# Decode attention with a gated MLP: part of the w_out matrix moved into a second transfer for partitions 0 to 31, and two products made 512 wide

## The chip, the cores and the metric

The kernel runs on one core of one Trainium2 chip. The metric is device microseconds (us) of one execution; lower is better. The kernel before was measured in three runs: 684.73, 684.85 and 684.87 us, median 684.85 us. One more execution was recorded by the hardware profiler; its own time is 684.74 us, and its span from the first to the last instruction is 682.9 us.

## The reference

One token for each of 8 batches goes through grouped-query attention over a cache, and the result is gated by a small MLP. All data are float32. Cut to what matters:

```python
xn = layernorm(x)                                # x: 8 x 512
q  = (xn @ wq)                                   # wq: 512 x 4096, 32 heads of 128
s  = softmax(q k^T / sqrt(128)) v                # k, v cache: 8 batches x 8 kv heads x 4096 x 128
s  = s.reshape(8, 4096) @ wo                     # wo: 4096 x 512
z  = gelu(xn @ w_in)                             # w_in: 512 x 1792, two halves z1, z2 of 896
g  = w_sp * layernorm(z2) + b_sp                 # scalars, since the sequence is 1 long
y  = (z1 * g) @ w_out                            # w_out: 896 x 512 = 7 blocks of 128 rows
out = x + s * silu(y)
```

The two caches hold 268 MB, nearly all of the 291 MB that one execution reads.

## The kernel before, in words

All large arrays come in over one queue, issued by SP in program order, into three slots of 64 KB in each of the 128 partitions (the pool `ring`). The order is: `w_mlp` (w_in and w_out side by side, 42 KB a partition), `wq`, then for each of the 8 kv heads two halves of k and two of v, each a full slot of 8 MB. SP issues a load as soon as the slot that it will overwrite has been read for the last time. Because the slots take turns, the second half of k for head 0 goes into the slot that `w_mlp` had, and its load waits until the MLP has written `gate` (line 182); the first half of v for head 0 waits for the last product with `wq`.

The second half of v of the last head comes in four pieces of 2 MB, and then `wo` in the pieces of `WO_PIECES` (line 29), counted in blocks m of 128 rows of `wo`: 16, 8, 4, 2, 1 and 1 blocks, so that little is left to compute when the last piece lands. Two small transfers go over a queue of their own, issued by ACT: `x` (8 rows of 2 KB) and `side` (128 rows of 520 bytes).

TensorE works in four column groups of 32 columns at a time (`R * g`), so that four products with few columns run side by side. For scores (line 212) and values (line 255) each product moves 512 columns of k or v past a small stationary matrix. Every matmul of float32 shows as two records in the profile. After a batch of values, DVE picks the diagonal blocks (`o_all`, line 258), adds them (`o_sb`, line 260), and `combine` (line 264) puts them into `po`, which is copied to `oT` (line 300).

The MLP (lines 121 to 182) runs while the first k loads are in flight. Its hidden vector lies in four groups of 32 partitions with 256 columns each; two transposes (line 168) and two copies turn it into `hT`, whose 7 blocks of 128 rows are multiplied by the 7 blocks of w_out, each in four column groups of 128 output columns (28 matmuls, line 174). The sigmoid of the result, times the result, is `gate`.

The final product (lines 303 to 307) takes 32 blocks of `wo`: for each block m four matmuls of 128 output columns, one in each column group g, all summed into the PSUM tile `acc`: 128 matmuls, 256 records. Then DVE multiplies by `gate`, adds `x` (from `side`), and SP stores 64 KB. The order of instructions within an engine is set by a planner when the program is built; it may put a `combine` ahead of the next batch of values.

Of the kernel before, what the change touches and what calls it, by code (L numbers as in the profile page):

```python
# [8 lines left out]
F32 = mybir.dt.float32  # L9
# [4 lines left out]
P = 128  # L14
B, D = 8, 512
HKV, REP, S, DH = 8, 4, 4096, 128
NK = D // P
G = 4
J = S // (G * P)
R = 32  # L20
FH = 896
FQ = 256
NB = FH // P
# [2 lines left out]
HALF = B // 2  # L26
UNIT = 2 * G * 512
SLOT = HALF * UNIT
WO_PIECES = [(0, 16), (16, 24), (24, 28), (28, 30), (30, 31), (31, 32)]


@with_exitstack
def tile_gqa_gmlp_decode(ctx: ExitStack, tc: tile.TileContext, x, side, kT, v, wq, wo,
                         w_mlp, out):
    nc = tc.nc
    const = ctx.enter_context(tc.tile_pool(name="const", bufs=1))
    ring = ctx.enter_context(tc.tile_pool(name="ring", bufs=3))
    work = ctx.enter_context(tc.tile_pool(name="work", bufs=1))
    small = ctx.enter_context(tc.tile_pool(name="small", bufs=2))
    ps_fix = ctx.enter_context(tc.tile_pool(name="ps_fix", bufs=1, space=bass.MemoryType.PSUM))  # L40
    ps = ctx.enter_context(tc.tile_pool(name="ps", bufs=2, space=bass.MemoryType.PSUM))

    def slot():
        return ring.tile([P, SLOT], F32, name="slot")
# [5 lines left out]
    nc.scalar.dma_start(side_sb, side)  # L50

    mlp_slot = slot()
    n_in, n_mlp = NK * 2 * FH, NK * 2 * FH + NB * D
    nc.sync.dma_start(mlp_slot[:, :n_mlp], w_mlp)
    w_in_sb = mlp_slot[:, :n_in].rearrange("p (k n) -> p k n", k=NK)
    w_out_sb = mlp_slot[:, n_in:n_mlp].rearrange("p (j d) -> p j d", j=NB)
    spare = [n_mlp]

    def from_slot(rows, n):
        lo = spare[0]  # L60
        spare[0] = lo + n
        return mlp_slot[:rows, lo:lo + n]
# [6 lines left out]
    ident = const.tile([P, P], F32, name="ident")  # L69
# [7 lines left out]
    same = const.tile([P, G, R], F32, name="same")  # L77
# [11 lines left out]

    sc = ps_fix.tile([P, 2, 512], F32, name="sc")  # L90
    o_ps = [ps_fix.tile([P, G, DH], F32, name=f"o_ps{i}") for i in range(2)]
    acc = ps_fix.tile([P, P], F32, name="acc")
    po_ps = ps_fix.tile([P, 2, B * REP], F32, name="po_ps")
    for t in (o_ps[0], o_ps[1], acc):
        nc.vector.memset(t, 0.0)

    def scratch(shape, name):
        t = ps.tile([P, 512], F32, name="scr")
        n = 1
        for s in shape[1:]:  # L100
            n *= s
        return t[:shape[0], :n]
# [16 lines left out]
    gate = const.tile([P, P], F32, name="gate")  # L119

    def mlp():
        z = from_slot(P, 2 * FQ).rearrange("p (a f) -> p a f", a=2)
        u = from_slot(P, 2 * FQ).rearrange("p (a f) -> p a f", a=2)
        pz = scratch([P, 2 * FQ], "pz")
        nc.vector.memset(pz, 0.0)
        for part in range(2):
            for k in range(NK):
                for g in range(G):
                    lo = g * FQ
                    n = min(FQ, FH - lo)  # L130
                    nc.tensor.matmul(pz[R * g:R * (g + 1), part * FQ:part * FQ + n], xnT[:, k, :],  # L131
                                     w_in_sb[:, k, part * FH + lo:part * FH + lo + n],
                                     start=(k == 0), stop=(k == NK - 1))
        zf, uf = z.rearrange("p a f -> p (a f)"), u.rearrange("p a f -> p (a f)")
        nc.vector.tensor_copy(zf, pz)
        nc.vector.tensor_mul(uf, zf, zf)
        nc.vector.tensor_scalar(uf, uf, 0.044715, 1.0, op0=ALU.mult, op1=ALU.add)
        nc.vector.tensor_mul(uf, uf, zf)
        nc.scalar.activation(uf, uf, AF.Tanh, scale=GELU_C)
        nc.vector.tensor_scalar(uf, uf, 1.0, 0.5, op0=ALU.add, op1=ALU.mult)  # L140
        nc.vector.tensor_mul(zf, uf, zf)

        def mean(src, name):
            part_sum = small.tile([P, 1], F32, name="part_sum")
            nc.vector.tensor_reduce(part_sum, src, op=ALU.add, axis=AX.X)
            pm = scratch([P, 1], "pm")
            nc.tensor.matmul(pm, same_all, part_sum, start=True, stop=True)
            t = small.tile([P, 1], F32, name=name)
            nc.vector.tensor_scalar(t, pm, 1.0 / FH, None, op0=ALU.mult)
            return t  # L150

        z1, z2 = z[:, 0, :], z[:, 1, :]
        mu = mean(z2, "mu")
        nc.vector.tensor_scalar(z2, z2, mu, None, op0=ALU.subtract)
        nc.vector.tensor_mul(u[:, 0, :], z2, z2)
        nc.vector.memset(u[(G - 1) * R:, 0, FH - (G - 1) * FQ:], 0.0)
        var = mean(u[:, 0, :], "var")
        nc.vector.tensor_scalar(var, var, EPS, None, op0=ALU.add)
        rs = small.tile([P, 1], F32, name="rs")
        nc.gpsimd.tensor_tensor(rs, var, neg_half, op=ALU.pow)  # L160
        nc.vector.tensor_scalar(z2, z2, rs, None, op0=ALU.mult)
        nc.vector.tensor_scalar(z2, z2, side_sb[:, P:P + 1], side_sb[:, P + 1:P + 2],
                                op0=ALU.mult, op1=ALU.add)
        nc.vector.tensor_mul(u[:, 1, :], z2, z1)
        hT = from_slot(P, 2 * P).rearrange("p (a s) -> p a s", a=2)
        for a in range(2):
            th = scratch([P, P], "th")
            nc.tensor.transpose(th, u[:, 1, a * P:(a + 1) * P], ident)
            nc.vector.tensor_copy(hT[:, a, :], th)
        py = scratch([P, P], "py")  # L170
        for j in range(NB):
            g0, a = divmod(j, 2)
            for g in range(G):
                nc.tensor.matmul(py[R * g:R * (g + 1), :], hT[:, a, R * g0:R * (g0 + 1)],  # L174
                                 w_out_sb[:, j, g * P:(g + 1) * P],
                                 start=(j == 0), stop=(j == NB - 1))
        e = from_slot(P, P)
        nc.vector.tensor_scalar(e, py, -1.0, 87.0, op0=ALU.mult, op1=ALU.min)
        nc.scalar.activation(e, e, AF.Exp)
        nc.vector.tensor_scalar(e, e, 1.0, None, op0=ALU.add)  # L180
        nc.vector.reciprocal(e, e)  # L181
        nc.vector.tensor_mul(gate, py, e)
# [22 lines left out]
    oT = const.tile([P, HKV, REP, B], F32, name="oT")  # L205
# [65 lines left out]
    def load_v(h, half, parts):  # L271
# [4 lines left out]
        return t.rearrange("p (i j e) -> p i j e", i=HALF, j=J)  # L276

    mlp()
    project_q(0)
    project_q(1)  # L280
    for h in range(HKV):
        for half in range(2):
            scores(h, half, load_k(h, half))
        pT = softmax(h)
        po = po_ps[:, h % 2]
        for half in range(2):
            last = h == HKV - 1 and half == 1
            v_sb = load_v(h, half, HALF if last else 1)
            if last:
                wo_slot = slot()  # L290
                for lo, hi in WO_PIECES:
                    nc.sync.dma_start(wo_slot[:, lo * D:hi * D], wo[:, lo * D:hi * D])
# [7 lines left out]
        nc.vector.tensor_copy(oT[:, h], po.rearrange("p (b r) -> p r b", r=REP))  # L300

    wo_sb = wo_slot.rearrange("p (m d) -> p m d", d=D)
    for m in range(HKV * REP):
        h, r = divmod(m, REP)
        for g in range(G):
            nc.tensor.matmul(acc[R * g:R * g + B, :], oT[:, h, r, :], wo_sb[:, m, g * P:(g + 1) * P],  # L306
                             start=(m == 0), stop=(m == HKV * REP - 1))

    res = const.tile([P, P], F32, name="res")
    nc.vector.tensor_mul(res, acc, gate)  # L310
# [37 lines left out]
```

## Time and profile before

| what | value |
|---|---|
| median of three runs | 684.85 us |
| time of the profiled execution | 684.74 us |
| its span | 682.9 us |
| busy PE, PEld, DVE | 373.4, 120.0, 172.1 us |
| data moved | 291.25 MB, mean 426 GB/s |
| share of queue q1 (all SP loads) in the time of the 16 DMA engines | 98.7% |
| product with wo (line 306), 256 records | 10.1 us busy, in the last 11 us |
| product with w_out (line 174), 56 records | 3.2 us busy, 32.6 to 35.8 us |
| store of the result, issue to landing | 1.6 us |

PE is TensorE's matmul row, PEld its weight loads, DVE the vector engine, SP the engine that issues the loads. In a group of instructions the columns are line, engine and operation, what is written and read, the shape, and the count; then busy time, mean duration in ns, and the idle time before them with what ended it. The clock that the throttle granted to TensorE is given in shares of full speed; in this kernel it is either 1.0 or 0.5, in stretches of 7 to 17 us.

The trace holds each DMA packet with its start, duration, size and queue, and each transfer's 16 completion events, one for each DMA engine. It does not name the engine of a packet. But the packets of one engine follow each other without a gap (the next starts 4 ns before the one before it ends), so that 16 chains can be followed from end to start through the span.

### The profile page before, as it was taken

How to read it: one execution, taken by the hardware profiler on the slowest of the kernel's cores; microseconds unless marked ns; L12 is line 12 of the kernel's file. 1: busy time of each engine (PE TensorE's matmuls, PEld its weight loads, DVE VectorE, ACT ScalarE, POOL GpSimd, SP SyncE). 2: the span in 40 equal slices, each digit the busy share in tenths (PEclk: the TensorE clock that was granted, in tenths of full speed). 3: DMA queues.
4: the chain of work that ended last, by engine and by line, in shares of the span. 5: the costliest groups of instructions: out<-in, count | busy, mean ns of one | idle time of the engine just before them, and what ended most of it. 6: DMA issues, size and time to landing. Idle time of an engine off the chain costs nothing.

```text
span 682.9 us, 6041 instructions
## 1 busy us (share of the span) xinstructions
PE 373.4 (55%) x2730; PEld 120.0 (18%) x2730; DVE 172.1 (25%) x370; ACT 13.5 (2%) x27; POOL 3.7 (1%) x11
## 2 busy tenths in 40 slices
PE   0455565447665455546665355556654454655676
PEld 0221121102111121112111011111211121111224
DVE  2440043302440033402431024401521024400441
ACT  0000000000000000000000000000000000000000
POOL 1000000000000000000000000000000000000000
PEclk9787768766777777777778777776777777766776
DMA  9999999999999999999999999999999999999996
GB/s 389 430 431 431 434 446 434 439 441 427 430 427 430 427 430 427 441 427 438 439 430 431 441 434 431 435 430 435 434 431 442 430 431 430 427 427 430 417 432 245
DMA packets 6521, 291.25 MB, mean 426 GB/s; under 512 B 728, under 2 KB 984, under 8 KB 1376
## 3 DMA queue, kind: packets, MB, share of 16 engines
q1 hardware_dynamic: 6336, 290.79, 98.7%
q8 instruction: 21, 0.34, 0.2%
q10 hardware_dynamic: 160, 0.08, 0.0%
q14 instruction: 4, 0.03, 0.0%
HBM read 290.80 MB, written 0.07 MB: 426 GB/s over the span
## 4 chain that ended last, share of the span: by engine, by line
DMA 72%; PE 19%; issue 4%; another core or an unknown queue 3%; DVE 2%; POOLq 0%; POOL 0%; ACT 0%; SPq 0%
DMA slot<-in_v 34%; DMA slot<-in_kT 33%; PE o_ps L255 9%; PE sc L212 9%; DMA slot<-in_wo 4%; PE po_ps L264 1%; PE scr L174 0%; DVE o_sb L260 0%; PE scr L243 0%; DMA x_sb<-in_x 0%; DVE o_all L258 0%; DVE nm L217 0%; DVE slot L181 0%; DVE p L238 0%
## 5 line engine op out<-in xcount | busy, mean ns | idle before, releaser
L212 PE MATMUL sc<-slot,qz 128*32 128x512 f32 x1024 | 147.8, 742 | 142.4 <-DMA slot<-in_kT 142.4
L255 PE MATMUL o_ps<-slot,pT 128*16 128x512 f32 x1024 | 154.0, 743 | 73.9 <-DMA slot<-in_v 73.9
L258 DVE TENSOR_TENSOR o_all<-o_ps,diag 128x512 f32<-128x512 f32 x64 | 44.2, 691 | 150.6 <-PE o_ps L255 150.5
L217 DVE TENSOR_REDUCE nm<-sc 128x1 f32<-128x1024 f32 x8 | 9.8, 1225 | 286.9 <-PE sc L212 286.9
L212 PEld LDWEIGHTS sc<-slot,qz 128*32 128x32 f32 x1024 | 36.0, 133 | 247.8 <-DMA slot<-in_kT 140.2
L260 DVE TENSOR_REDUCE o_sb<-o_all 128x128 f32<-128x512 f32 x64 | 67.9, 1061 | 2.2
L255 PEld LDWEIGHTS o_ps<-slot,pT 128*16 128x16 f32 x1024 | 30.0, 112 | 155.0 <-issue 105.4
L264 PE MATMUL po_ps<-fold,o_sb 128*128 128x4 f32 x128 | 25.0, 266 | 28.0 <-DVE o_sb L260 27.9
L264 PEld LDWEIGHTS po_ps<-fold,o_sb 128*128 128x128 f32 x128 | 19.4, 191 | 73.8 <-DVE o_sb L260 73.8
L243 PE MATMUL scr<-ident,p 128*128 128x128 f32 x64 | 15.2, 418 | 10.7 <-DVE p L238 10.7
L219 ACT ACTIVATE p<-sc,nm 128x1024 f32<-128x1024 f32 x8 | 8.9, 1114 | 584.5 <-DVE nm L217 584.5
L245 DVE COPY pT<-scr 128x128 f32<-128x128 f32 x64 | 13.9, 284 | 9.9 <-PE scr L243 9.9
L243 PEld LDWEIGHTS scr<-ident,p 128*128 128x128 f32 x64 | 12.3, 219 | 11.1 <-issue 11.1
L306 PE MATMUL acc<-slot,oT 128*8 128x128 f32 x256 | 10.1, 326 | 1.6 <-DMA slot<-in_wo 1.6
L131 PE MATMUL scr<-slot,xnT 128*32 128x256 f32 (+1 forms) x64 | 5.0, 451 | 10.7 <-DMA slot<-in_w_mlp 10.7
L222 PE MATMUL scr<-ident,nm 128*1 128x128 f32 x8 | 2.2, 270 | 10.9 <-DVE nm L217 10.9
L306 PEld LDWEIGHTS acc<-slot,oT 128*8 128x8 f32 x256 | 7.3, 105 | 4.2 <-DMA slot<-in_wo 2.2
L189 PE MATMUL scr<-slot,xnT 128*32 128x512 f32 x64 | 7.5, 609 | 0.0
L235 PE MATMUL scr<-wl,same 128*128 128x1 f32 x16 | 3.6, 297 | 6.2 <-DVE wl L233 6.2
L238 DVE TENSOR_SCALAR p<-p,w 128x1024 f32<-128x1024 f32 x8 | 6.0, 753 | 0.3
L131 PEld LDWEIGHTS scr<-slot,xnT 128*32 128x32 f32 x64 | 2.9, 138 | 12.4 <-issue 11.8
L201 DVE COPY qz<-scr 128x4 f32<-128x4 f32 x64 | 4.6, 152 | 1.5 <-PE scr L195 1.5
(74 smaller groups left out, 56.3 us busy)
## 6 DMA issues: line engine op xcount, KB each, us to landing
slot<-in_v SPq DMA_DIRECT2D x4, 2048.0 KB, 41.0
slot<-in_w_mlp SPq DMA_DIRECT2D x1, 5376.0 KB, 15.4
slot<-in_wo SPq DMA_DIRECT2D x1, 4096.0 KB, 38.5
slot<-in_wo SPq DMA_DIRECT2D x1, 2048.0 KB
slot<-in_wo SPq DMA_DIRECT2D x1, 1024.0 KB, 45.1
slot<-in_wo SPq DMA_DIRECT2D x1, 512.0 KB, 37.9
slot<-in_wo SPq DMA_DIRECT2D x2, 256.0 KB, 31.6
slot<-in_kT SPq DMA_DIRECT2D x16, 48.3
```

Source lines behind the costliest of these rows:

```text
L131: nc.tensor.matmul(pz[R * g:R * (g + 1), part * FQ:part * FQ + n], xnT[:, k, :], w_in_sb[:, k, part * FH + lo:part * FH + lo + n], start=( ...
L189: nc.tensor.matmul(pq[R * g:R * (g + 1), :], xnT[:, k, :], wq_sb[:, k, lo:lo + REP * DH], start=(k == 0), stop=(k == NK - 1))
L212: nc.tensor.matmul(sc[R * g:R * (g + 1), c, :], qz[:, h, b * R:(b + 1) * R], k_sb[:, i, c, g, :], start=(b == 0), stop=(b == B - 1))
L217: nc.vector.tensor_reduce(m, sc, op=ALU.max, axis=AX.XY, negate=True)
L219: nc.scalar.activation(p.rearrange("p j s -> p (j s)"), sc.rearrange("p c s -> p (c s)"), AF.Exp, bias=m, accum_out=l[:, h:h + 1])
L243: nc.tensor.transpose(t[:, j * P:(j + 1) * P], p[:, 4 * c + j, :], ident)
L245: nc.vector.tensor_copy(pT[:, 4 * c + j].rearrange("p b (g r) -> p g b r", g=G), t[:, j * P:(j + 1) * P].rearrange("p (g b r) -> p g b r", ...
L255: nc.tensor.matmul(of[R * c:R * c + G * REP, :], pT[:, j, b, :], v_unit[:, j], start=(j < G), stop=(j >= J - G))
L258: nc.vector.tensor_mul(o_all, o, diag[:, :, None].to_broadcast([P, G, DH]))
L260: nc.vector.tensor_reduce(o_sb, o_all.rearrange("p g d -> p d g"), op=ALU.add, axis=AX.X)
L264: nc.tensor.matmul(po[:, b * REP:(b + 1) * REP], o_sb, fold, start=True, stop=True)
L306: nc.tensor.matmul(acc[R * g:R * g + B, :], oT[:, h, r, :], wo_sb[:, m, g * P:(g + 1) * P], start=(m == 0), stop=(m == HKV * REP - 1))
```

## The change

There are three parts.

1. The weights of the MLP are split. `w_mlp` keeps w_in and the w_out blocks 0, 2, 4 and 6 (6 KB a partition fewer, in all 128 partitions). The blocks 1, 3 and 5 go into a new array `w_low` as quarters of 32 rows: 32 rows of 24 KB, written as 8 groups of 4 rows with 256 bytes of padding behind each group. One transfer issued by ACT, behind `x` and `side`, brings them to partitions 0 to 31. The bytes moved are the same.
2. The product with w_out is made 512 columns wide: one transpose and one copy for the four even blocks (4 matmuls), four transposes and one copy for the quarters (12 matmuls with 32 rows), summed in `pw`; the partial sums lie in four row groups and are copied to SBUF and folded by 4 matmuls with `same`. Some buffers of the MLP move from the slot to the tiles `p` and `pT`.
3. `wo` comes in seven pieces (8, 8, 8, 4, 2, 1, 1 blocks). The blocks 0 to 27 are multiplied 512 columns wide, one matmul for each block, four blocks side by side in the column groups; the sum is copied to SBUF and folded into `acc` by 4 matmuls. The last 4 blocks go the old way, two ahead of the fold and two behind it. `part` and `acc` reuse the PSUM of the scores.

```diff
-WO_PIECES = [(0, 16), (16, 24), (24, 28), (28, 30), (30, 31), (31, 32)]
+WO_PIECES = [(0, 8), (8, 16), (16, 24), (24, 28), (28, 30), (30, 31), (31, 32)]
+FOLDED = HKV * REP - REP
+QR = P // 4
+LOW_E = 8
+N_LOW = (NB - G) * 4 * D
...
-    n_in, n_mlp = NK * 2 * FH, NK * 2 * FH + NB * D
+    n_in, n_mlp = NK * 2 * FH, NK * 2 * FH + G * D
+    n_low = n_mlp + N_LOW
     nc.sync.dma_start(mlp_slot[:, :n_mlp], w_mlp)
...
+    nc.scalar.dma_start(mlp_slot[:QR, n_mlp:n_low],
+                        w_low[:, :P // (4 * LOW_E) * N_LOW].rearrange("e (i n) -> e i n", n=N_LOW))
...
-    for t in (o_ps[0], o_ps[1], acc):
+    for t in o_ps:
...
-        for a in range(2):
-            th = scratch([P, P], "th")
-            nc.tensor.transpose(th, u[:, 1, a * P:(a + 1) * P], ident)
-            nc.vector.tensor_copy(hT[:, a, :], th)
+        nc.tensor.transpose(th, u[:, 1, :P], ident)
+        nc.vector.tensor_copy(hT, th)
+        tl = scratch([QR, 4 * P], "tl")
+        for a in range(4):
+            nc.tensor.transpose(tl[:, a * P:(a + 1) * P], u[:, 1, P + a * QR:P + (a + 1) * QR], ident)
+        nc.vector.tensor_copy(hL.rearrange("p a s -> p (a s)"), tl)
+        pw = scratch([P, D], "pw")
+        for g in range(G):
+            nc.tensor.matmul(pw[R * g:R * (g + 1), :], hT[:, R * g:R * (g + 1)], w_out_sb[:, g, :],
+                             start=True, stop=(g == G - 1))
+        for a in range(4):
+            for g in range(NB - G):
+                nc.tensor.matmul(pw[R * g:R * (g + 1), :], hL[:, a, R * g:R * (g + 1)],
+                                 w_low_sb[:, g, a, :], start=False, stop=(a == 3))
+        nc.vector.tensor_copy(y_sb, pw)
         py = scratch([P, P], "py")
-        for j in range(NB):
-            g0, a = divmod(j, 2)
-            for g in range(G):
-                nc.tensor.matmul(py[R * g:R * (g + 1), :], hT[:, a, R * g0:R * (g0 + 1)],
-                                 w_out_sb[:, j, g * P:(g + 1) * P],
-                                 start=(j == 0), stop=(j == NB - 1))
+        for g in range(G):
+            nc.tensor.matmul(py[R * g:R * (g + 1), :], same[:, 0, :], y_sb[:, g * P:(g + 1) * P],
+                             start=True, stop=True)
...
-    for m in range(HKV * REP):
+    part, acc = sc[:, 0, :], sc[:, 1, :P]
+    for m in range(FOLDED):
         h, r = divmod(m, REP)
-        for g in range(G):
-            nc.tensor.matmul(acc[R * g:R * g + B, :], oT[:, h, r, :], wo_sb[:, m, g * P:(g + 1) * P],
-                             start=(m == 0), stop=(m == HKV * REP - 1))
+        nc.tensor.matmul(part[R * r:R * r + B, :], oT[:, h, r, :], wo_sb[:, m, :],
+                         start=(m < REP), stop=(m >= FOLDED - REP))
+    part_sb = work.tile([P, D], F32, name="part_sb", tag="p")
+    nc.vector.tensor_copy(part_sb, part)
+
+    def last_head(lo, hi):
+        for m in range(lo, hi):
+            h, r = divmod(m, REP)
+            for g in range(G):
+                nc.tensor.matmul(acc[R * g:R * g + B, :], oT[:, h, r, :], wo_sb[:, m, g * P:(g + 1) * P],
+                                 start=(m == FOLDED), stop=(m == HKV * REP - 1))
+
+    last_head(FOLDED, FOLDED + 2)
+    for g in range(G):
+        nc.tensor.matmul(acc[R * g:R * g + B, :], same[:, 0, :B], part_sb[:, g * P:(g + 1) * P],
+                         start=False, stop=False)
+    last_head(FOLDED + 2, HKV * REP)
...
+    w2 = c(B_w_out).reshape(NB, P, D)
+    rows = P // (4 * LOW_E)
+    low = np.zeros((LOW_E, rows * N_LOW + 64), np.float32)
+    low[:, :rows * N_LOW] = w2[1::2].reshape(NB - G, 4, LOW_E, rows, D).transpose(2, 3, 0, 1, 4).reshape(LOW_E, -1)
```

More of the change, by code (lines that the diff above doesn't have):

```diff
@@ L28 @@
 SLOT = HALF * UNIT
-WO_PIECES = [(0, 16), (16, 24), (24, 28), (28, 30), (30, 31), (31, 32)]
+WO_PIECES = [(0, 8), (8, 16), (16, 24), (24, 28), (28, 30), (30, 31), (31, 32)]
[3 more added lines that the diff above has]
+N_LOW = (NB - G) * 4 * D
 @with_exitstack
 def tile_gqa_gmlp_decode(ctx: ExitStack, tc: tile.TileContext, x, side, kT, v, wq, wo,
-                         w_mlp, out):
+                         w_mlp, w_low, out):
     nc = tc.nc
@@ L52, in tile_gqa_gmlp_decode @@
     mlp_slot = slot()
-    n_in, n_mlp = NK * 2 * FH, NK * 2 * FH + NB * D
+    n_in, n_mlp = NK * 2 * FH, NK * 2 * FH + G * D
+    n_low = n_mlp + N_LOW
     nc.sync.dma_start(mlp_slot[:, :n_mlp], w_mlp)
     w_in_sb = mlp_slot[:, :n_in].rearrange("p (k n) -> p k n", k=NK)
-    w_out_sb = mlp_slot[:, n_in:n_mlp].rearrange("p (j d) -> p j d", j=NB)
-    spare = [n_mlp]
+    nc.scalar.dma_start(mlp_slot[:QR, n_mlp:n_low],
+                        w_low[:, :P // (4 * LOW_E) * N_LOW].rearrange("e (i n) -> e i n", n=N_LOW))
+    w_out_sb = mlp_slot[:, n_in:n_mlp].rearrange("p (j d) -> p j d", j=G)
+    w_low_sb = mlp_slot[:QR, n_mlp:n_low].rearrange("p (j a d) -> p j a d", a=4, d=D)
+    spare = [n_low]
     def from_slot(rows, n):
@@ L91, in tile_gqa_gmlp_decode @@
     o_ps = [ps_fix.tile([P, G, DH], F32, name=f"o_ps{i}") for i in range(2)]
-    acc = ps_fix.tile([P, P], F32, name="acc")
     po_ps = ps_fix.tile([P, 2, B * REP], F32, name="po_ps")
-    for t in (o_ps[0], o_ps[1], acc):
+    for t in o_ps:
         nc.vector.memset(t, 0.0)
@@ L121, in mlp @@
     def mlp():
-        z = from_slot(P, 2 * FQ).rearrange("p (a f) -> p a f", a=2)
-        u = from_slot(P, 2 * FQ).rearrange("p (a f) -> p a f", a=2)
+        zu = work.tile([P, 4, FQ], F32, name="zu", tag="p")
+        z, u = zu[:, :2], zu[:, 2:]
+        hy = work.tile([P, 2 * D], F32, name="hy", tag="pT")
+        y_sb, hL = hy[:, :D], hy[:QR, D:].rearrange("p (a s) -> p a s", a=4)
         pz = scratch([P, 2 * FQ], "pz")
@@ L164, in mlp @@
         nc.vector.tensor_mul(u[:, 1, :], z2, z1)
-        hT = from_slot(P, 2 * P).rearrange("p (a s) -> p a s", a=2)
-        for a in range(2):
-            th = scratch([P, P], "th")
-            nc.tensor.transpose(th, u[:, 1, a * P:(a + 1) * P], ident)
-            nc.vector.tensor_copy(hT[:, a, :], th)
-        py = scratch([P, P], "py")
-        for j in range(NB):
-            g0, a = divmod(j, 2)
-            for g in range(G):
-                nc.tensor.matmul(py[R * g:R * (g + 1), :], hT[:, a, R * g0:R * (g0 + 1)],
-                                 w_out_sb[:, j, g * P:(g + 1) * P],
-                                 start=(j == 0), stop=(j == NB - 1))
+        hT = from_slot(P, P)
+        th = scratch([P, P], "th")
+        nc.tensor.transpose(th, u[:, 1, :P], ident)
[13 more added lines that the diff above has]
+        nc.vector.tensor_copy(y_sb, pw)
+        py = scratch([P, P], "py")
+        for g in range(G):
+            nc.tensor.matmul(py[R * g:R * (g + 1), :], same[:, 0, :], y_sb[:, g * P:(g + 1) * P],
+                             start=True, stop=True)
         e = from_slot(P, P)
@@ L336 @@
             c(B_w_in).reshape(NK, P, 2 * FH).transpose(1, 0, 2).reshape(P, NK * 2 * FH),
-            c(B_w_out).reshape(NB, P, D).transpose(1, 0, 2).reshape(P, NB * D)], axis=1),
+            w2[0::2].transpose(1, 0, 2).reshape(P, G * D)], axis=1),
+        "w_low": low,
     }
```

## The prediction

> **What bounds the kernel now.** I read the page's DMA slices and queues first, then the end of the chain of work that ended last, the timeline and clock of the last 25 us, SP's own waits, and last the single packets and completion events.
>
> ```profile
> span 682.9 us, 6041 instructions
> ...
> DMA  9999999999999999999999999999999999999996
> ...
> q1 hardware_dynamic: 6336, 290.79, 98.7%
> q8 instruction: 21, 0.34, 0.2%
> q10 hardware_dynamic: 160, 0.08, 0.0%
> q14 instruction: 4, 0.03, 0.0%
> ```
> ```profile
> 649.78 29.43 DMA slot<-in_wo
> 679.21 0.04 issue
> 679.25 0.45 PE acc L306 x8
> 679.70 0.02 issue
> 679.72 0.30 DVE res L310
> ```
>
> The DMA engines are busy in every slice, q1 alone for 98.7% of their time. The landing of the last wo piece at 679.21 sets the end; 8 TensorE records, two DVE operations and the store follow. A change can move only that landing or what is left behind it.
>
> The transfers give the cause of 679.21. A packet of 65,536 bytes takes 2.418 us on every engine, all span long (tenth to ninetieth percentile 2.418 to 2.427). Yet the 16 completions of the last wo piece come at 674.16, .22, .23, .34, .46, .56, .63 (seven engines), 677.36, .41, .61, .64, .74 (five) and 678.85, .90, 679.19, .21 (four). Followed packet by packet, the delays are the instruction packets of q8 and q14: a q8 packet (16,384 bytes) costs its engine 1.50 to 1.56 us, a q14 packet (8,192 bytes) 0.95 to 0.98. The q8 packets go round eight chains, two or three times each. The three q14 packets ahead of the end (47, 210 and 516 us) all fall on a ninth chain, which I call the odd one: 3.2 us late, completion 677.41. Seven chains get none.
>
> ```profile
> 667.33 0.59 PE L264 MATMUL po_ps<-fold,o_sb 128*128 128x4 f32 x2 [1.87 <-DVE o_sb L260]
> ...
> 669.31 9.70 PE L306 MATMUL acc<-slot,oT 128*8 128x128 f32 x248 [1.40 <-DMA slot<-in_wo]
> ...
> 679.25 0.40 PE L306 MATMUL acc<-slot,oT 128*8 128x128 f32 x8 [0.24 <-DMA slot<-in_wo]
> ```
> ```profile
> 669.30:674.40 5.10, 5.09 (x98) 3.63 (x101) 0.00 (x0) 0.00 (x0) 0.00 (x0) 0.50 0.96 392
> 674.40:677.90 3.50, 3.50 (x133) 3.10 (x124) 0.00 (x0) 0.00 (x0) 0.00 (x0) 1.00 0.49 192
> ```
>
> TensorE is nearly a second bound: it waits for wo from 667.9 to 669.31, then works without a break until 677.9, half of it at clock 0.50, and only the last four blocks wait for their data.
>
> **The transfer w_low.** It takes 3 blocks x 2 KB = 6 KB from each of the 128 rows of w_mlp: 8 rows an engine, 49,152 bytes. From the pitches of packets (65,536 bytes every 2.414 us, 32,768 every 1.21) an engine moves 27.2 bytes a ns, so every engine gains 1.81 us. The 768 KB come back in 32 rows. Which engines carry them? `x`, also 8 groups on ACT's queue, left 8 packets of 2,048 bytes and 8 completions on 8 engines. Five of these run straight into a first w_mlp packet and so can be placed: all five are chains without q8 packets. So I take the eight of `x` as the half that q8 leaves alone: the seven early chains and the odd one. If w_low takes the same eight, each gets 98,304 bytes, 3.61 us, plus 4 packets' gaps and a completion, 0.03: net +1.84 us; the other eight get -1.81.
>
> At the end: the seven land at 674.63 + 1.84 = 676.47 at the latest, the q8 chains at 679.21 - 1.81 = 677.40, the odd chain at 677.41 + 1.84 = 679.25. The odd chain takes the place of the slowest, 0.04 us behind it. The eight that were late gain 1.8 us and nobody is left to use it.
>
> A rule speaks against the transfer as such: the Trainium skill, "DMA: Bandwidth & Descriptors", section "Rules for kernel authors", asks for all 16 engines and warns that a small outermost dimension confines a transfer to few. By it the 1.84 us would be a loss, landing 681.05; the completions above show seven of the eight engines some 5 us early, so here the price is 0.04.
>
> **The piece of wo split in two.** 16 rows an engine of 16,384 bytes (0.610 pitch) for 8 of 32,768 (1.21): 9.76 - 9.68 = +0.08 us with the completion, on all engines; landing 679.33. SP issues one more load; these issues wait for transfers eight back:
>
> ```profile
> SPq L268 <- DVE gate L182: 36.1, 1, 36.1
> SPq L292 <- DMA slot<-in_v: 17.1, 3, 8.0
> ```
>
> With one piece more, the last one waits for the last v piece (659.55) and stands 18 us ahead of its data: nothing. The store, queued behind it on SP, waits for DVE anyway.
>
> **The MLP.** The w_out product becomes 10 sets of four (or three) records side by side. Values, also 512 wide, start such sets 0.44 us apart at clock 1.0 and 0.85 at 0.5, so 4.4 to 8.5 us for 3.21; copies of 0.69 (two of 512 columns), three more transposes and a fold add 1.5 to 2, and the low engines' w_mlp lands 1.5 to 1.9 us later. `gate` comes 4 to 10 us after its 38.11. Queued behind is SP's load of the second k half (the first line above) and everything that SP issues after it, and project_q on TensorE, so the first v load and the first scores also. The queue holds k's first half until 54.0: cover 15.9 us, above the upper end. From scores on each load has a slot's time, 19.3 us, in hand. Nothing reaches the end. DVE's instructions come out even (a memset and two copies against four copies), so its packets stay where they are.
>
> **The product with wo.** 256 records become 96; with the MLP's -13, 173 pairs or 346 TensorE instructions fewer. q8 packets come every 254 instructions in the mean (193 to 300 from one to the next), so one or two fewer of 21, at the very end: the one at 673.1 falls late or away, on a chain that has 1.8 us to spare then. Nothing.
>
> On TensorE a block costs the same: four records side by side, 0.109 us a set at clock 1.0 and 0.213 at 0.5 for 128 columns, two sets a block; 512 wide, two sets of 0.43 or 0.85 for four blocks. So 0.22 or 0.43 us a block either way. What changes is the order. Piece 0 to 8 (landing near 664.6) is there when values end at 667.95; 16 blocks at 0.43 end by 674.8; the next 8 (landed 674.4) by 676.5 at clock 1.0; blocks 24 to 27, landing near 676.8 on the odd chain, end at 677.75 with the pipeline. Then a new chain: part_sb, 128x512 from PSUM, 0.69 as line 135's copy, done 678.5; fold, 0.22, done 678.8, with blocks 28 and 29 (landing 678.0) ahead of it; block 30 (678.7) done 679.0; block 31 at 679.33. So 0.3 us are to spare, and from the landing on the tail is the old one, 0.45 us of TensorE and DVE and store unchanged: +0.0. At clock 0.5 through blocks 24 to 31: 676.8 + 1.8 + 0.75 + 0.43 + 0.86 = 680.6 against 679.8: +0.8, the upper end.
>
> **Sum.** 0.04 + 0.08 + 0.0 = +0.12 us on the profiled 684.74: 684.86. That run stands 0.11 below the median of 684.85, so the forecast is 685.0. I call within 0.2% (1.37 us) no change; a measurement of this kernel tells about that.
>
> **Rivals.**
> - Faster: the odd chain is not the last, because it is not among w_low's eight, or its three q14 packets spread over other engines. For: only five of `x`'s eight engines could be placed; the odd one is in by exclusion. Against: the q8 round has exactly eight members, and it is none of them. Then the q8 chains set the end at 677.40 + 0.08 = 677.48; blocks 24 to 27 land at 675, so TensorE keeps up; 684.74 - 1.73 = 683.0.
> - Slower, by the clock: it stays at 0.5 to the end. For: TensorE starts 1.4 us earlier into a stretch of 0.5 that began at 657.3. Against: that one already lasted 17.1 us, the longest of all. 24 blocks then end at 678.2, 27 at 679.9, part_sb 680.65, fold 681.1, block 31 at 682.0 against 679.70: 687.1. It decides once 1.0 comes later than about 680.
> - Slower, by the low half: w_low costs its engines over 3.1 us more (fewer than eight engines, or packets slower than 27.2 bytes a ns), or the odd chain gets one more instruction packet. On four engines the transfer costs 7.2 us instead of 3.6: 688.5; with low engines as late as the others, the full 1.84 us would show: 686.6. The completions speak against the one, and no row shows a slower packet past the first 3 us of the span. The 686.6 is what the Trainium skill's rule on all 16 engines, above, would make of it.
> - The split has no effect: w_low goes over all 16 engines and landing stays at 679.29: 684.9, no change either.
>
> **Chances.** My forecast 0.58, no effect 0.08: within 0.2%, 0.66. Faster 0.17. Slower 0.17 (clock 0.09, low half 0.08). The forecast's own range is 684.7 to 685.8. The range takes in the faster rival at 683.0 with its spread, and half of the small slips that stay below the slower ones: 682.9 to 686.2.
>
> **What would show it.** The last wo piece's 16 completions: one alone near 679.3, eight at 675.5 to 677.5, seven at 676.0 to 676.5. The load from in_w_low: 32 packets of 24,576 bytes on eight chains without q8 packets. The first k load behind `gate` issued at 42 to 49, DMA slices still at 9. Part_sb's copy done near 678.5, the fold before block 31. I am wrong if the last completion is near 677.5, if the fold ends behind it, or if a DMA slice falls below 9 before the last.

## The result and the profile after

The changed kernel takes 685.9 us (median of 22 runs, 685.02 to 687.51); beside it the kernel before took 684.87 us (22 runs, 684.62 to 685.07). The ratio is 1.0016, 95% interval 1.0009 to 1.0022: slower by 0.16%, inside the 0.2% that the prediction called no change, and inside its range of 682.9 to 686.2. The forecast was 685.0.

The median hides what is new: the runs of before lie within 0.45 us, those of after form two clusters, nine runs at 685.02 to 685.26 and ten at 686.41 to 687.51, with three in between (685.76 to 686.03). The profiled execution, 687.51 us, is the slowest one. The page after, its span, slices and queues:

```profile
span 685.7 us, 5701 instructions
...
DMA  9999999999999999999999999999999999999994
...
q1 hardware_dynamic: 6480, 290.00, 98.1%
q10 hardware_dynamic: 200, 0.87, 0.3%
q8 instruction: 20, 0.33, 0.2%
q14 instruction: 4, 0.03, 0.0%
```

The engines are still never idle, 0.79 MB went from q1 to q10, and one instruction packet of q8 is gone. The end of the chain of work that ended last (start, us, what):

```profile
632.37 43.81 DMA slot<-in_wo
676.19 0.04 issue
676.23 4.38 PE sc L324 x24
680.61 0.02 issue
680.63 0.70 DVE part_sb L327
681.33 0.04 issue
681.38 0.62 PE sc L333 x16
682.00 0.22 PE sc L338 x8
682.22 0.48 PE sc L333 x16
```

The path no longer ends on the last landing. The chain starts at the piece of blocks 16 to 23 (landed at 676.19) and goes on through the wide product, the copy `part_sb` and the fold. Blocks 24 to 27, whose piece landed at 678.63, start at 678.67 and end at 680.61, at clock 0.5. The 16 completions of the last wo piece, from the trace, of before and of this execution:

```
before  674.16 .22 .23 .34 .46 .56 .63 | 677.36 .41 .61 .64 .74 | 678.85 .90 | 679.19 .21
after   672.50 673.06 | 675.66 .74 .88 .88 676.04 .07 .24 .40 .52 | 677.19 .55 | 679.44 | 681.11 .20
```

The last landing is 1.99 us later, and TensorE ends 1.50 us behind it (682.70) where it ended 0.49 behind it before: 3.0 us later in all; the spans differ by 2.9, the store and what follows it being 0.1 shorter. In the early part, the timeline:

```profile
14.59 5.65 PE L140 MATMUL scr<-slot,xnT 128*32 128x256 f32 x64 [8.46 <-DMA slot<-in_w_mlp]
...
35.04 7.04 PE L188 MATMUL scr<-slot,hy 32*32 32x512 f32 x24 [1.23 <-DMA slot<-in_w_low]
...
45.51 0.29 DVE L200 TENSOR_TENSOR gate<-scr,slot 128x128 f32<-128x128 f32 x1
```

The MLP begins 1.7 us earlier than before (smaller w_mlp), waits 1.2 us for w_low, and ends 7.7 us later (45.80 for 38.11); the DMA slices show no gap from it.

Which engines are last? Followed packet by packet (the engine of a packet is inferred from packets that follow each other without a gap), w_low is 32 packets of 24,576 bytes, each 0.912 us, four on each of eight chains. Of these eight, one has the q14 packets (54, 212, 518 us; in this profile its chain touches another's near 200 us, in the later ones, where it does not, all three lie on one low engine; a fourth, at 660.5, lies on another and delays none of the last), and two belong to the round of q8, with three packets each (47, 302, 587 and 63, 341, 628 us). The other six members of the round are not among w_low's eight; of the engines outside w_low's eight, two serve no instruction packets at all: 672.50 and 673.06.

### The profile page after: what moved, and what is told of

Same layout as the page of the kernel before. It is cut to its first block, busy times and chain, and to the rows that moved or that the text cites. A ratio compares the mean times of both kernels' runs of the same rounds, so it can differ in the third digit from the quotient of the medians.

```text
span 685.7 us, 5701 instructions
## 1 busy us (share of the span) xinstructions
PE 379.4 (55%) x2557; PEld 113.3 (17%) x2557; DVE 173.8 (25%) x371; ACT 13.5 (2%) x27; POOL 3.7 (1%) x11
## 4 chain that ended last, share of the span: by engine, by line
DMA 81%; PE 17%; DVE 1%; issue 0%; ACTq 0%; SPq 0%
DMA slot<-in_kT 35%; DMA slot<-in_v 35%; PE sc L230 7%; PE o_ps L273 6%; DMA slot<-in_wo 6%; DMA slot<-in_w_low 5%; PE scr L207 1%; PE scr L188 1%; PE sc L324 1%; PE po_ps L282 0%; DVE o_sb L278 0%; DVE o_all L276 0%; PE sc L333 0%; SPq L310 0%; DVE q_sb L210 0%
## 5 line engine op out<-in xcount | busy, mean ns | idle before, releaser
L273 PE MATMUL o_ps<-slot,pT 128*16 128x512 f32 x1024 | 152.1, 734 | 75.0 <-DMA slot<-in_v 75.0
L324 PE MATMUL sc<-slot,oT 128*8 128x512 f32 x56 | 9.4, 800 | 3.2 <-DMA slot<-in_wo 3.2
L188 PE MATMUL scr<-slot,hy 32*32 32x512 f32 x24 | 7.0, 1055 | 1.2 <-DMA slot<-in_w_low 1.2
```

Source lines behind the costliest of these rows:

```text
L188: nc.tensor.matmul(pw[R * g:R * (g + 1), :], hL[:, a, R * g:R * (g + 1)], w_low_sb[:, g, a, :], start=False, stop=(a == 3))
L273: nc.tensor.matmul(of[R * c:R * c + G * REP, :], pT[:, j, b, :], v_unit[:, j], start=(j < G), stop=(j >= J - G))
L324: nc.tensor.matmul(part[R * r:R * r + B, :], oT[:, h, r, :], wo_sb[:, m, :], start=(m < REP), stop=(m >= FOLDED - REP))
```

## The experiments

**Theory A**: w_low's eight engines, which I call the low ones, include engines that serve instruction packets; these get 1.84 us on top and set the end. Which q8 member gets a third packet depends on where the round begins, and that makes two clusters. **Rival B**: the fold behind block 27 costs the time. **Rival C**: the longer MLP holds up the queue. (A lower-cluster execution never came up under the profiler, see below.)

### The changed kernel again

> The changed kernel once more, on the chip of the other three. Theory A (w_low's eight engines hold three that also serve instruction packets): the last wo piece completes on one low engine with three q14 packets near 679.4, and on two low engines with q8 packets near 681.2 if they got three each, near 679.6 if they got two; time 685.0 with two, 686.5 to 687.5 with three. Rival B (the new fold behind block 27 is the cost): the time follows the gap from the last completion to the end of TensorE's work, 0.5 us before and 1.5 us in the profile of after, and not the completions. Rival C (the longer MLP holds up the queue): a DMA slice below 9 before the last, and all sixteen completions late together.

Measured: 685.97 us, median of 10 runs, five at 685.19 to 685.52 and five at 686.42 to 687.40; ratio to the kernel before, measured beside it, 1.0017 (95% interval 1.0008 to 1.0026; so also below). The profiled execution took 686.70 us. Of the two low members of the round one has three q8 packets (47, 302, 587 us), the other two; the three latest completions are 679.49, 679.50 and 681.21. That is A to 0.1 us; 679.5 is where the q14 engine and a low engine with two q8 packets land. The chain's end:

```profile
678.70 1.09 PE sc L324 x8
...
679.81 0.70 DVE part_sb L327
...
681.18 0.22 PE sc L338 x8
681.40 0.48 PE sc L333 x16
```

TensorE ends at 681.88, 0.67 behind the last landing: the tail does cost, but 0.2 us here and 1.0 us in the first profile. The difference is the clock, the rows of which I read in the trace: 0.5 from 677.5 to 680.9 there; the 24 records of blocks 16 to 27 end at 680.61 there and 679.79 here.

### Product of wo alone, and division alone

The third part without the others, against the kernel before:

```diff
-WO_PIECES = [(0, 16), (16, 24), (24, 28), (28, 30), (30, 31), (31, 32)]
+WO_PIECES = [(0, 8), (8, 16), (16, 24), (24, 28), (28, 30), (30, 31), (31, 32)]
+FOLDED = HKV * REP - REP
...
+        nc.tensor.matmul(part[R * r:R * r + B, :], oT[:, h, r, :], wo_sb[:, m, :],
+                         start=(m < REP), stop=(m >= FOLDED - REP))
...
```

> The kernel before with the third part alone: seven wo pieces, wide product, fold. A: completions as before plus 0.08 us, time 684.9 with a tail of 0.5 us, at most 685.9 with a tail of 1.5. B: 685.9, as after. C: 684.9.

Measured: 685.07 us (11 runs, ten at 684.86 to 685.18, one at 685.89), ratio 1.0003 (0.9994 to 1.0012). One cluster. The last completion is 679.31 (679.21 before), the tail 0.64 us:

```profile
677.89 0.70 DVE part_sb L309
678.59 0.04 issue
678.63 0.62 PE sc L315 x16
679.25 0.22 PE sc L320 x8
679.47 0.48 PE sc L315 x16
```

The first products behind the copy are those of blocks 28 and 29. Their piece had landed at 678.00, but TensorE stands idle until the copy is done and begins at 678.63; from there the fold and the last blocks follow without a gap to 679.95, 0.64 behind the last landing for 0.49 before.

Parts one and two without the third, against the changed kernel (`WO_PIECES` as before too):

```diff
+    for m in range(HKV * REP):
+        h, r = divmod(m, REP)
+        for g in range(G):
+            nc.tensor.matmul(acc[R * g:R * g + B, :], oT[:, h, r, :], wo_sb[:, m, g * P:(g + 1) * P],
+                             start=(m == 0), stop=(m == HKV * REP - 1))
-    for m in range(FOLDED):
...
```

> The changed kernel with the old product with wo and its old six pieces: parts one and two alone. A: low engines late as in after (679.3, or 681.1 with three q8 packets), time 684.9 to 686.6 with the old tail of 0.5 us. B: 684.9, as before. C: as after.

Measured: 11 runs, seven at 684.85 to 685.21 and four at 686.31 to 686.75, median 685.13; ratio 1.001 (1.0001 to 1.0018). Two clusters without any fold. The profiled execution (686.31 us) has its last completion at 680.84 and the old tail:

```profile
650.34 30.50 DMA slot<-in_wo
680.84 0.04 issue
680.88 0.45 PE acc L324 x8
```

So the clusters come with parts one and two, and B is not the main cost; what the wide product adds by itself is a tenth or two. The medians of these kernels depend on how many runs fall into each cluster, so that the clusters have to be compared and not the medians.

### The fold earlier

```diff
-FOLDED = HKV * REP - REP
+FOLDED = HKV * REP - 2 * REP
...
-    last_head(FOLDED, FOLDED + 2)
+    last_head(FOLDED, FOLDED + REP)
     # fold
-    last_head(FOLDED + 2, HKV * REP)
+    last_head(FOLDED + REP, HKV * REP)
```

> The changed kernel with the fold one head earlier: blocks 0 to 23 wide and folded, 24 to 31 the old way, the fold between blocks 27 and 28. A (low engines with instruction packets): the two clusters of times stay, near 685.0 to 685.2 and near 686.5, since the completions do not change; only the third step, 687.4 in after, goes away, which is a tail at clock 0.5. B (the fold is the cost): all runs at 684.9, one cluster.

Measured: 686.56 us (11 runs, 685.09 to 688.60; two of them below 685.3), ratio 1.0023 (1.0014 to 1.0032). In the profile the tail is the old one, and the last completion still 681.25:

```profile
656.66 24.59 DMA slot<-in_wo
681.25 0.04 issue
681.29 0.45 PE sc L333 x8
```

B falls as the cause of the clusters: with the fold off the path the upper one stays near 686.5. My expectation that nothing above 686.6 would be left missed: 687.31 and 688.60 are in the list, and no profile shows why.

### w_low over all sixteen engines

```diff
-    nc.scalar.dma_start(mlp_slot[:QR, n_mlp:n_low],
-                        w_low[:, :P // (4 * LOW_E) * N_LOW].rearrange("e (i n) -> e i n", n=N_LOW))
+    nc.scalar.dma_start(mlp_slot[:QR, n_mlp:n_low], w_low)
...
-    low = np.zeros((LOW_E, rows * N_LOW + 64), np.float32)
-    low[:, :rows * N_LOW] = w2[1::2].reshape(NB - G, 4, LOW_E, rows, D).transpose(2, 3, 0, 1, 4).reshape(LOW_E, -1)
+    low = c(w2[1::2].reshape(NB - G, 4, QR, D).transpose(2, 0, 1, 3)).reshape(QR, N_LOW)
```

> The changed kernel with w_low as 32 plain rows without padding, so that all 16 engines carry it; nothing else is changed. A: the two groups of engines lie together again, last completion 679.2 to 679.5, time 684.8 to 685.9 by what the fold leaves behind it. B: last completion near 679.3 as well, but the tail stays what it is in after, and the time goes down by no more than the completions do: 685.9 if the tail is 1.5 us. C: time as after, since the MLP is as long.

Measured: 689.92 us (5 runs, 689.21 to 690.36), ratio 1.0073 (1.0059 to 1.0087). A miss of every theory. The bytes do lie evenly now, two rows an engine, and the completions of the last piece spread over 5.2 us (679.23 to 684.46), about as in before (5.05), but all of them are 5 us late. The stretch of 17 to 26 us, while w_low is under way, in all16 and in the changed kernel (busy times, then granted clock, DMA share, GB/s):

```profile
17.00:26.00 9.00, 4.01 (x45) 1.89 (x37) 4.04 (x7) 0.63 (x1) 0.00 (x0) 0.86 1.07 277
```
```profile
17.00:26.00 9.00, 3.67 (x43) 1.98 (x37) 4.20 (x8) 0.63 (x1) 0.00 (x0) 0.97 0.98 423
```

The engines are as busy and move a third less. A w_low packet takes 1.15 to 2.10 us (median 1.57) instead of 0.912, and the packets of 65,536 bytes that start between 20 and 26 us a median of 4.11 us instead of 2.418. So this could not test A, but showed something else, which the next one asks about.

### w_low into other rows

```diff
+LO = 64
...
-    nc.scalar.dma_start(mlp_slot[:QR, n_mlp:n_low],
+    nc.scalar.dma_start(mlp_slot[LO:LO + QR, n_mlp:n_low],
...
-    y_sb, hL = hy[:, :D], hy[:QR, D:].rearrange("p (a s) -> p a s", a=4)
+    y_sb, hL = hy[:, :D], hy[LO:LO + QR, D:].rearrange("p (a s) -> p a s", a=4)
```

> The changed kernel with w_low written to partitions 64 to 95 instead of 0 to 31; the same 8 groups and so the same low engines, the weights of the quarters' product in the same rows. It tells what slowed all16, where packets of 65,536 bytes took 4.1 us instead of 2.4 beside w_low. If it is the count of engines on one small transfer: as after, packets of 24,576 bytes take 0.91 us. If it is which engine writes which rows (two engines into the same rows' path): packets take up to twice as long beside it, and the end is 2 to 5 us later than after.

Measured: 693.05 us (4 runs, 691.90 to 694.68), ratio 1.0121 (1.0107 to 1.0135). The same 8 groups, on eight engines, four packets each; only the rows differ. Packets of w_low take 1.25 to 1.79 us (median 1.70), and those of 65,536 bytes 3.05 to 4.18 us until 36 us. The two stretches of it that answer to those above:

```profile
17.00:26.00 9.00, 4.01 (x44) 1.83 (x35) 4.04 (x7) 0.63 (x1) 0.00 (x0) 0.87 0.98 293
26.00:36.00 10.00, 4.31 (x17) 1.87 (x17) 4.00 (x12) 0.00 (x0) 0.56 (x1) 0.50 0.97 288
```

The end is later than expected: the last completion is at 687.23, 6 us behind that of after, for 2 to 5. So it is not the count of engines. What fits the three kernels is that a small transfer is cheap if each engine writes the rows that it writes in the large transfers as well, and dear if it does not, for itself and for the engines that it meets. The trace does not name rows and engines, so the pairing itself is not shown by it. The Trainium skill, "DMA: Bandwidth & Descriptors", section "The descriptor swizzle", gives the pairing: in a transfer to 128 partitions an engine writes four neighbouring partitions and the four that lie 32 above, engines 0 to 7 those below 64, each through one port. By it, if the eight groups go to engines 0 to 7 in order, which no trace shows, 8 groups of 4 rows in partitions 0 to 31 fall exactly on their own engines, and neither the 16 pairs of rows of all16 nor the rows 64 to 95 of rows64 do; the three measurements agree with it.

### More bytes on the low engines

```diff
+            nc.scalar.dma_start(more, w_low[:, :4 * 448].rearrange("e (i n) -> e i n", n=448))   # behind the softmax of heads 0 to 6
```

> The changed kernel with seven more transfers of the form of w_low, one behind each softmax, 32 rows of 1,792 bytes in 8 groups, into a tile that nothing reads: 28 packets more on each of the low engines, about 0.075 us each, 2.1 us in all, none on the others. A: the low engines set the end, so everything moves by 2.1 us: 687.1 in the lower cluster, 688.6 to 689.5 in the upper one. B and C: the two halves average out or the tail sets the end: under 1 us more.

Measured: 721.46 us (5 runs, 721.13 to 721.87), ratio 1.0534 (1.0520 to 1.0549). The experiment failed as a test of A: the planner moved the small transfers ahead of the MLP's work on ACT, where each waits for the one before:

```profile
DMA  9983199999999999999999999999999999999996
```
```profile
65.68 1.28 ACT L148 ACT_TABLE_LOAD   x1 [65.68 <-DMA more<-in_w_low]
...
88.40 0.29 DVE L200 TENSOR_TENSOR gate<-scr,slot 128x128 f32<-128x128 f32 x1
```

It shows C's mechanism where it does decide: `gate` at 88.7 instead of 45.8, far past the 54 us until which k's first half lasts, and the slices fall to 1. In after they stay at 9; C falls for the change itself.

### A third of the dose

One block of w_out in w_low instead of three; the blocks 1 and 3 stay in w_mlp as full blocks and are multiplied from a second transpose.

```diff
-N_LOW = (NB - G) * 4 * D
+N_FULL = G + 2
+N_LOW = 4 * D
...
-    n_in, n_mlp = NK * 2 * FH, NK * 2 * FH + G * D
+    n_in, n_mlp = NK * 2 * FH, NK * 2 * FH + N_FULL * D
```

> The changed kernel with one block of w_out in w_low instead of three (blocks 1 and 3 go back into w_mlp), so that the low engines carry 0.61 us more than the mean and the others 0.61 less, instead of 1.84 and 1.81. A: from the completions of after, the odd engine at 678.2, a low engine with three q8 packets at 679.9 to 680.0, with two at 678.4, the others with three at 678.7; so two clusters again, 684.2 to 684.5 and 685.4 to 685.7, both below after's by 0.7 to 1.2 us. B (fold): times as after, 685.1 to 687.4. No effect of the division: as the kernel with the product of wo alone, 685.0.

Measured: 11 runs, three at 684.04 to 684.16, one at 685.09 and seven at 685.27 to 686.21; median 685.39, ratio 1.0004 (0.9995 to 1.0013). In the profile (685.64 us) the completions end with 678.05, 678.29, 680.04 and 680.05; expected were 678.2 to 678.7 and 679.9 to 680.0. The times are less exact: the lowest three lie 0.1 us under the lower cluster as expected (684.2 to 684.5), and the seven spread wider than the upper one (685.4 to 685.7). The latest completions follow the dose of the low engines: 681.2 at +1.84 us, 680.05 at +0.61. The lowest runs, 684.04 to 684.16, beat every run of before; most do not.

### Three more profiles of the changed kernel

> One more profile of the changed kernel. A: its time follows from where the round of q8 packets begins. If the two low engines of the round are among the first three or four, one of them has three packets and the last completion is at 681.2, time 686.5 or more; if not, it is at 679.4 to 679.7 and the time is 685.0 to 685.3. B: the time follows the clock at the end alone.

> One more profile of the changed kernel, to meet an execution of the lower cluster. A: at 685.0 to 685.3 no low engine has three q8 packets ahead of the end and the last completion is at 679.4 to 679.7, on the engine of q14 or a low one with two q8 packets; at 686.4 or more one of the low engines is at 681.1 to 681.3. B: the same completions in both clusters.

> As after_look2: last completion 679.4 to 679.7 at a time of 685.0 to 685.3, 681.1 to 681.3 at 686.4 or more.

Measured: 686.61, 686.69 and 686.61 us, all in the upper cluster. In each of the three profiles two low engines of the round have three q8 packets each, and the last two completions are 681.06 and 681.13, 681.20 and 681.21, 680.80 and 681.13. In all five profiles of the changed kernel the round begins on a low engine. The completions of a lower-cluster execution were therefore not seen; that both low members then got two packets is inferred from the 679.5 in after_again, which with the tail gives 685.0 to 685.2, and not shown. What sets the beginning of the round is open.

The clock alone, B of the first of these expectations, does not make the upper cluster: in four of the five profiles it is 1.0 from 675.1 us at the latest until TensorE is done, and the time is still 686.6 to 686.7. It does account for the step above, 687.51 with 0.5 from 677.5 to 680.9. The three runs between the clusters would fit the early landing with such a tail; no profile shows one.

## Why the prediction was right, and which step was wrong

**What bounds the kernel** held: DMA slices at 9 to the end, rigid packets of 2.418 us, lateness from instruction packets. The fold came behind the last landing, which the prediction named as a way to be wrong, and does now share the bound.

**The transfer w_low**: it went over eight engines, four packets of 24,576 bytes each, and I take them to be those of `x`. The shift is as worked out: the completions of wq are 33.28 to 33.85 on the eight others and 36.85 to 37.32 on the low ones, 3.6 us apart in the mean (worked out 3.65); in the kernel before they all lie at 35.01 to 35.49. The odd chain was among them and completed at 679.44 in the profile of after; forecast 679.33.

**The step that failed** is "So I take the eight of `x` as the half that q8 leaves alone". The round's eight members are two of w_low's eight engines and six of the others. Five of `x`'s engines could be placed; the other three were filled in by exclusion, and two of them were wrong. So the list of who is late lacked two engines at up to 676.5 + 4.65 = 681.1 (three q8 packets of 1.55 each), where 681.2 was measured. The faster rival rested on the same exclusion from the other side. The mechanism was priced (low engines that are as late as the others lose the full 1.84: "686.6", with 0.08 for all of that rival) but with too small a chance: about half of the executions are there, at 686.4 to 687.5. The lower cluster lies at 685.0 to 685.5, where the forecast had put the odd chain.

**The rule on all sixteen engines** from the Trainium skill, "DMA: Bandwidth & Descriptors", section "Rules for kernel authors", was weighed as a loss of 1.84. The loss did show, in the upper cluster, near the 686.6 that the prediction gave for it. As a remedy the rule fails here, and the measurement decides: w_low over sixteen engines gave 689.92 us, over eight 685.97 beside it. The rival "The split has no effect", 684.9 with w_low on all engines, was wrong with it by 5 us: it took an even load for a free one.

**The MLP**: `gate` 7.7 us later, forecast 4 to 10, hidden as said. One part went the other way: w_mlp did not land 1.5 to 1.9 us later but 1.65 earlier (14.46 for 16.11), since it is 6 KB a partition smaller and w_low was not under way beside it: the rows of `side` stand ahead of w_low on ACT's queue, and w_low's packets run from 18.3 us on, among those of wq, and land at 32.0 to 34.9. The fourth q14 packet came at 660.5 instead of 682.0, so not all of these packets stayed where they were; it made no engine the last.

**The product with wo**: q8 packets 20 for 21, as said. +0.0 for the tail was too little: wo_only shows 0.64 us for 0.49. There the copy is done at 678.59, as forecast, but blocks 28 and 29, which the prediction had run beside it, wait for it. `part` and `acc` are two parts of one tile, `sc`; whether the wait comes from that was not tested. In the changed kernel part_sb's copy is done at 680.4 to 681.3 instead of 678.5 where the low engines' piece for blocks 24 to 27 completes at 678.65 instead of 676.8. The first profile, with clock 0.5 there, has the +0.8 of the upper end and 0.2 more. The split of the piece cost 0.10 us in wo_only's last completion; forecast 0.08. The seventh load did not wait for the last v piece but for the third (issued at 656.61 in after), and was far ahead of its data all the same.

**Sum**: forecast +0.12 us on the profiled execution; the lower cluster's +0.2 to +0.4 on before's median agrees with that and 0.2 us of tail; the upper cluster has 1.5 to 2.6 us, of which the last landing is 1.9 to 2.0 in the profiles and the tail 0.2 to 1.0. The median, 685.9, lies between the clusters, where few executions are. That it falls into the range of 682.9 to 686.2 is partly luck: the working fits the lower cluster, and the upper one lies outside the range.

## What to carry to other kernels

When a kernel is bound by DMA engines that never idle, the end belongs to the latest engine, and bytes moved between engines pay only if one knows which engines are late: list every engine with its delays, and do not fill in the list by symmetry. A delay whose place changes between executions cannot be balanced by a fixed division; here it made one steady time into two. A small transfer to a part of the partitions may cost more over sixteen engines than over eight; by the three kernels here it should be cut so that each engine writes the rows that it writes in the large ones.

## What the runs showed of the hardware that was not expected

- The packets of the instruction queue q8, 16,384 bytes each, come one for about 254 TensorE instructions (253.7 in the mean in before, 252.1 in after), and each costs one of the 16 engines 1.50 to 1.56 us. The round has eight members, two of them among the eight engines that an 8-group transfer uses, and begins at different members: on a low one in all five profiles of the changed kernel, on one of the others in split_only and rows64.
- The same 768 KB took 0.91 us a packet in rows 0 to 31 over eight engines, 1.57 in these rows over sixteen and 1.70 in rows 64 to 95 over eight, in the last two with packets of 65,536 bytes beside it at up to 5.1 and 4.2 us instead of 2.42. That engines slow each other where they write rows that are not theirs is inferred from this.
